# Attention and two MLPs in one kernel: q's two score parts made in place and carried by transfers, v's load later, a third column buffer

## The chip, the cores and the metric

The kernel runs on one core of a Trainium2 chip. The metric is the device time of one execution in microseconds; where several were taken, their median. A core has TensorE (PE, with its weight loads PEld), VectorE (DVE), ScalarE (ACT), GpSimd (POOL) and SyncE (SP), which here only issues transfers (DMAs). Each engine works through its own row of instructions in order; semaphores make one wait for another.

## The reference: what is computed

Rotary attention over 4 x 8 heads, 576 positions, 64 numbers a head, and two MLPs over the 2304 rows that it gives:

```python
q_rot, k_rot = (rotate(q), rotate(k))
scores = scale * np.matmul(q_rot, k_rot.transpose(0, 1, 3, 2))      # scale = 1/8
attn = np.exp(scores - np.max(scores, axis=-1, keepdims=True))
attn = attn / (np.sum(attn, axis=-1, keepdims=True) + 1e-09)
x = np.matmul(attn, v)                              # -> 2304 x 512
...
h = x @ w_in
g = np.where(h >= 1, h, np.where(h <= -1, 0.0, (h + 1) ** 2 / 4))
x = g @ w_out                                       # 512 -> 2048 -> 512
...
g = s * np.maximum(x @ w_in2, 0.0) ** 2 + b
out = g @ w_out2
```

## The kernel before

**Pairs and units.** Two heads share the 128 partitions, 64 each, so the 32 heads make 16 pairs. A pair is worked through in 9 units (`UNITS`). A unit makes scores of 128 rows by 576 columns on TensorE (`qk`, L352) in one of two score buffers (`ps_s`, `sc`), VectorE takes the row maximum (L354, `nm`), ScalarE the exponential (L359, `p`), which frees the score buffer. Two units later TensorE transposes `p` (L374), and later multiplies it with v (`av`).

**Two parts.** The scores are made with 32-bit numbers cut in two: a high part that TensorE takes as it is, and the rest. For q, both parts of a head stand above each other in one tile `qs` of 128 partitions: high part of head 0 in the lower half, its rest in the upper half, and for head 1 the other way round. Beside it stands k: `kh` holds k's high part twice, `kz` its rest.

**q before the change** (`rope_pair`, `lay_q`): the load `qin` brings q and its swapped halves side by side (`t[:, 0]`, `t[:, 1]`). GpSimd multiplies both by the table of cosines and sines (L96, in four pieces), VectorE adds them (L293). Then for each head, on its 64 partitions, ScalarE writes the scaled high part straight into `qs` (L306), and VectorE the rest into the other half of `qs` (L307): two instructions on each engine for a pair. There are two `qs` tiles, used in turn, so these writes wait until the scores two pairs earlier have been made.

**k** already goes the way that q takes after the change: parts are made in place in `kin` (L318 on ScalarE, L96 on GpSimd), and six transfers of 64 partitions on SP carry them to `kh` and `kz` (L323, L324).

**What sets the order.** Four buffers (`QB`) hold `qin` and `kin`; the one of a pair is loaded again for the pair two later. The code names in which unit a step is asked for (`do_load`): q of the next pair in unit 0, k in unit 2, v in unit 3, the loads of q and k for the pair after it in units 4 and 6. The framework's scheduler then sorts each engine's row by a time line of its own, so a step can stand far from there. All transfers are issued by SP, in one row: one that has to wait holds all behind it.

**Beside the pairs.** From about the fourth pair on, ScalarE, VectorE and GpSimd convert the weights of the first MLP from raw 64-bit form (`wraw`, L144, L133 to L138), and from the sixth pair on chunks of that MLP run beside the pairs (`beside`, L180): their columns come through the buffers `xs` (`split_x`), of which there are two. After the last pair the MLP stages fill the rest of the span.

Of the kernel before, what the change touches and what calls it, by code (L numbers as in the profile page):

```python
# [8 lines left out]
F32 = mybir.dt.float32  # L9
F32R = mybir.dt.float32r  # L10
# [3 lines left out]
AF = mybir.ActivationFunctionType  # L14
ALU = mybir.AluOpType
# [8 lines left out]
P = 128  # L24
# [37 lines left out]
N1 = 288  # L62
# [4 lines left out]
def kernel(ctx, tc, qq, kk, vv, tab, ww1, ww2, s, b, out):  # L67
    nc = tc.nc
# [31 lines left out]
    def split(dst_hi, dst_lo, src, hi_eng, lo_eng):  # L100
        if hi_eng is nc.scalar:
            made.append(nc.scalar.copy(dst_hi, src).ins)
        else:
            hi_eng.tensor_copy(dst_hi, src)
        tt = pool_tt if lo_eng is nc.gpsimd else nc.vector.tensor_tensor
        tt(out=dst_lo, in0=src, in1=dst_hi, op=ALU.subtract)  # L106
# [7 lines left out]
    class Slice:  # L114
# [6 lines left out]
        def convert(self, raw, pools, hi, lo):  # L121
            if not wide:
                split(hi, lo, raw, nc.scalar, nc.gpsimd)
                return


            top = raw.bitcast(F32).rearrange("p (n t) -> p n t", t=2)[:, :, 1]
            low = raw.bitcast(U16).rearrange("p (n t) -> p n t", t=4)[:, :, 1]
            pool = pools[self.f * 2 + self.made & 1 if len(pools) > 1 else 0]
            a = pool.tile([P, HW], F32, tag="wa", name="wa", bufs=WB)  # L130
            m = pool.tile([P, HW], F32, tag="wm", name="wm", bufs=WB)
            au, mu = a.bitcast(U32), m.bitcast(U32)
            nc.scalar.activation(a, top, AF.Copy, scale=2.0 ** -112)  # L133
            nc.vector.tensor_scalar(out=mu, in0=au, scalar1=3, scalar2=None, op0=ALU.logical_shift_left)
            nc.vector.scalar_tensor_tensor(out=mu, in0=au, scalar=0x80000000, in1=mu, op0=ALU.bitwise_and, op1=ALU.bitwise_or)
            nc.vector.tensor_scalar(out=au, in0=mu, scalar1=0xFF800000, scalar2=None, op0=ALU.bitwise_and)
            nc.vector.scalar_tensor_tensor(out=a, in0=low, scalar=2.0 ** -36, in1=a, op0=ALU.mult, op1=ALU.mult)
            nc.scalar.copy(hi, m)  # L138
            pool_tt(out=m, in0=m, in1=hi, op=ALU.subtract)
            pool_tt(out=lo, in0=m, in1=a, op=ALU.add)  # L140
# [95 lines left out]
    m2 = p1.enter_context(tc.tile_pool(name="m2", bufs=2, reuse_waits="tile"))  # L236
# [20 lines left out]
    def load_qk(i, nm, pieces=WHOLE):  # L257
        bb, hp = divmod(i, NP)
        t = att2.tile([P, 2, S], F32, tag="qkin", name=f"{nm}in", bufs=QB)
        for c in pieces:  # L260
            nc.sync.dma_start(out=t[:, :, c], in_=(qq if nm == "q" else kk)[bb, hp, :, :, c])
        qk_in[nm, i] = t

    def load_v(i):
        bb, hp = divmod(i, NP)
        t = att2.tile([P, 5, 2, D], F32, tag="vin", name="vin", bufs=VB)
        for out, src in ((t[:, :, 1], vv[bb, hp, :, :, 1]), (t[:D, :4, 0], vv[bb, hp, D:, :4, 0]), (t[D:, :4, 0], vv[bb, hp, :D, 1:, 0]), (t[D:, 4, 0], vv[bb, hp, :D, 0, 0])):
            nc.sync.dma_start(out=out, in_=src)
        v_in[i] = t
# [7 lines left out]
    QW = S + 2 * D  # L277
# [7 lines left out]
    def rope_pair(i, nm, mul, add, lo_eng, pieces=WHOLE):  # L285

        t = qk_in.pop((nm, i))
        tt = {nc.gpsimd: pool_tt, nc.vector: nc.vector.tensor_tensor}
        last = None
        for c in pieces:  # L290
            tt[mul](out=t[:, :, c], in0=t[:, :, c], in1=tab_sb[:, :, c], op=ALU.mult)
            r = t[:, 1, c]
            tt[add](out=r, in0=t[:, 0, c], in1=r, op=ALU.add)  # L293
            last = (lay_q if nm == "q" else lay_k)(i, t, c, lo_eng)
        return last

    SELF = [slice(0, D), slice(D, P)]

    def lay_q(i, t, c, lo_eng, heads=range(2)):

        st = stacks["q", i] = qs_t[i % 2]
        r = t[:, 1, c]
        for j in heads:
            own, other = SELF[j], SELF[1 - j]
            at = slice(j * QW + c.start, j * QW + c.stop)
            h = nc.scalar.activation(st[own, at], r[own], AF.Copy, scale=0.125)  # L306
            m = nc.vector.scalar_tensor_tensor(out=st[other, at], in0=r[own], scalar=0.125, in1=st[own, at], op0=ALU.mult, op1=ALU.subtract)  # L307
        return h.ins, m.ins
# [144 lines left out]
    def load_parts(x, n0, n):  # L453

        for t in range(2):
            nc.sync.dma_start(out=x[t].bitcast(F32), in_=parts_at(t, n0, n))
        return x

    def split_x(c, again):
        xh = m1.tile([P, KD, N1], F32R, tag="xh", name="xh")  # L460
        xl = m1.tile([P, KD, N1], F32R, tag="xl", name="xl")
        if again:
            return load_parts((xh, xl), c * N1, N1)
        for k in range(KD):
            xs = m2.tile([P, N1], F32, tag="xs", name="xs", bufs=2)
            nc.sync.dma_start(out=xs, in_=xd[k, :, c * N1:(c + 1) * N1])
            split(xh[:, k, :], xl[:, k, :], xs, nc.scalar, nc.gpsimd)
        return xh, xl

    kept, begun = set(), set()  # L470

    def beside(work):
        x = split_x(work[0][0], work[0][0] in kept)
        for _ in range(LEAD):
            yield 1.0
        for n, (c, gi) in enumerate(work):
# [12 lines left out]
            if n + 1 < len(work) and work[n + 1][0] != c:  # L489
                x = split_x(work[n + 1][0], work[n + 1][0] in kept)  # L490
# [27 lines left out]
    def turned_by(t, c):  # L518
        nc.vector.tensor_tensor(out=t[:, :, c], in0=t[:, :, c], in1=tab_sb[:, :, c], op=ALU.mult)
        nc.vector.tensor_tensor(out=t[:, 1, c], in0=t[:, 0, c], in1=t[:, 1, c], op=ALU.add)  # L520
# [5 lines left out]
    lay_k(0, tk, HALVES[1], [nc.gpsimd, nc.gpsimd], [0])  # L526
    turned_by(tq, QP[0])
    hi, rest = lay_q(0, tq, QP[0], None, [0])
    with tc.issue_after(hi):
        first = lay_k(0, tk, HALVES[1], [nc.gpsimd, nc.gpsimd], [1])  # L530
    hi, rest = lay_q(0, tq, QP[0], None, [1])
    with tc.issue_after(first):
        load_qk(1, "k")
# [37 lines left out]
    def do_load(n):  # L571
        if n < 2:
            with tc.issue_after(maxs[0] if n else rest):
                turned_by(tq, QP[n + 1])
                lay_q(0, tq, QP[n + 1], None)
        if n < len(units):
            i, k = units[n]
            if i + 1 < NPAIR:
                if k == (i == 0):
                    with ExitStack() if i else tc.issue_after(maxs[1]):  # L580
                        rope_pair(i + 1, "q", nc.gpsimd if i else nc.vector, nc.vector, None)
                elif k == 2:
                    with ExitStack() if i else tc.issue_after(exps[2]):
                        rope_pair(i + 1, "k", nc.gpsimd, nc.gpsimd, [nc.gpsimd, nc.vector])
                elif k == 3:
                    load_v(i + 1)
                elif k in (4, 6) and i + 2 < NPAIR:
                    load_qk(i + 2, "q" if k == 4 else "k")

        if n in range(33, 51, 2) or n in range(70, 110, 4):  # L590
            with tc.issue_after(exps[n - 14]):
                convert()

        if n in PARK_AT and parking:
            with tc.issue_after(exps[n - 4]):
                parking.pop(0).park(wst, scratch)()
# [31 lines left out]
    def do_fill(n):  # L628
        if n < 48:
            return  # L630
        with tc.issue_after(exps[min(n, len(units)) - 4]):
            run_fill(0.62 if n < 76 else 0.92)

    acts = {"q": do_qk, "l": do_load, "t": do_t, "a": do_av, "f": do_fill}
    for n in range(len(units) + LA):
        with ExitStack() as st:
# [377 lines left out]
    def cut(n0, n1, n):  # L1014

        k = -(-(n1 - n0) // n)
        at = [n0 + (n1 - n0) // 16 * i // k * 16 for i in range(k + 1)]
        return [(a, b - a) for a, b in zip(at, at[1:])]
# [5 lines left out]
    a, b, c, d = cut(last, NT, N2A), cut(0, last, N2), cut(last, NT, N2), cut(0, NT, N2)  # L1024
# [153 lines left out]
```

## Time and profile before

| | |
|---|---|
| three runs | 1129.34, 1130.87, 1133.84 us; median 1130.87 |
| the profiled execution | 1128.27 us; its span 1126.5 us |
| PE busy | 1077.9 us (96%) |
| PEld busy | 986.6 us (88%) |
| DVE busy | 780.8 us (69%) |
| ACT busy | 631.7 us (56%) |
| POOL busy | 429.5 us (38%) |
| DMA queue of SP | 48.9% of 16 engines' span |

The span runs from the first to the last instruction of the profiled execution; the execution's own time has 1.8 us more around it. Busy shares are means over stages that have different limits, and a matmul's end is modelled, so a busy TensorE is not one at its peak. The pairs fill about the first 440 us.

### The profile page before, as it was taken

Reading aid. Unit: us, or ns where it says so; the run is one execution under the profiler, and the core shown is the slowest. Engines: PE = TensorE matmul, PEld = TensorE weight load, DVE = VectorE, ACT = ScalarE, POOL = GpSimd, SP = SyncE. Lnnn points to the kernel's source line nnn. Section 1 sums busy time; section 2 is a strip of 40 time slices with the busy share of each in tenths; the row PEclk is TensorE's granted clock in tenths of the full one; section 3 lists DMA queues with packets and bytes.
Section 4 is the critical chain, followed back from the end, with each engine's and each line's share of the span. In section 5 each row is a group of like instructions: output and inputs, shape, how many; then the busy total and the mean of one; then the engine's idle time right before and its main releaser. Section 6 shows DMA issues by size and latency. Waiting matters only on the chain.

```text
span 1126.5 us, 20041 instructions
## 1 busy us (share of the span) xinstructions
PE 1077.9 (96%) x7296; PEld 986.6 (88%) x7296; DVE 780.8 (69%) x1449; ACT 631.7 (56%) x1430; POOL 429.5 (38%) x564
## 2 busy tenths in 40 slices
PE   3999998989999999999999999999999999999998
PEld 3666677878988989999999999999999999999997
DVE  6888987775676663365656667766877678767754
ACT  4777776775766765554545545465444448334421
POOL 7969886885453241252544444310211120000000
PEclk9999998999999999999999999999999999999999
DMA  7565855665667552745466673322232754221220
GB/s 228 164 180 165 243 158 182 213 170 177 186 193 216 174 182 76 262 130 187 141 221 222 193 234 113 118 77 88 80 126 90 274 182 126 82 70 54 81 62 35
DMA packets 109762, 173.24 MB, mean 154 GB/s; under 512 B 29408, under 2 KB 80608, under 8 KB 109664
## 3 DMA queue, kind: packets, MB, share of 16 engines
q1 hardware_dynamic: 109664, 171.97, 48.9%
q8 instruction: 57, 0.93, 0.3%
q14 instruction: 41, 0.34, 0.1%
HBM read 110.10 MB, written 48.56 MB: 141 GB/s over the span
## 4 chain that ended last, share of the span: by engine, by line
PE 77%; DVE 5%; DMA 5%; POOL 4%; ACT 3%; issue 2%; SPq 1%; POOLq 0%; ACTq 0%
PE hps L180 15%; PE sum L914 13%; PE yps L830 6%; PE yps L828 6%; PE yps L829 6%; PE sc L352 5%; PE h L180 4%; PE yps L764 4%; PE yps L766 4%; PE yps L765 4%; PE y L180 4%; PE av L400 3%; PE tp L374 3%; POOL kin L96 2%; DMA kin<-in_k 1%
## 5 line engine op out<-in xcount | busy, mean ns | idle before, releaser
L180 PE MATMUL hps<-xh,w 128*128 128x288 f32 (+4 forms) x640 | 163.3, 324 | 0.0
L354 DVE TENSOR_REDUCE nm<-sc 128x1 f32<-128x576 f32 x144 | 107.9, 752 | 43.2 <-PE sc L352 42.5
L352 PE MATMUL sc<-kh,qs 128*128 128x288 f32 x336 | 104.7, 333 | 28.5 <-ACT p L359 16.6
L359 ACT ACTIVATE p<-sc,nm 128x576 f32<-128x576 f32 x144 | 106.8, 744 | 33.5 <-DVE nm L354 32.6
L830 PE MATMUL yps<-gh,w 128*128 128x480 f32 (+1 forms) x320 | 118.5, 370 | 0.0
L828 PE MATMUL yps<-gh,w 128*128 128x480 f32 (+1 forms) x320 | 118.4, 370 | 0.0
L829 PE MATMUL yps<-gl,w 128*128 128x480 f32 (+1 forms) x320 | 118.4, 370 | 0.0
L922 ACT ACTIVATE four<-four,b_sb,s_sb 128x480 f32<-128x480 f32 x64 | 47.4, 782 | 126.3 <-DVE four L921 126.3
L96 POOL TENSOR_TENSOR wm<-wm,w 128x256 f32<-128x256 f32 x80 | 71.3, 912 | 120.1 <-ACT w L138 74.2
L180 PEld LDWEIGHTS hps<-xh,w 128*128 128x128 f32 x640 | 113.3, 188 | 1.0
L352 PEld LDWEIGHTS sc<-kh,qs 128*128 128x128 f32 x336 | 65.2, 197 | 47.9 <-ACT p L359 24.5
L180 PE MATMUL hps<-xl,w 128*128 128x288 f32 (+4 forms) x320 | 103.6, 324 | 0.0
L352 PE MATMUL sc<-kz,qs 128*128 128x288 f32 x336 | 95.9, 305 | 0.0
L374 PE MATMUL tp<-ident,p 128*128 128x128 f32 x576 | 89.4, 280 | 5.4 <-ACT p L359 3.3
L764 PE MATMUL yps<-gh,w 128*128 128x288 f32 (+3 forms) x288 | 93.2, 324 | 1.1 <-ACT ys L502 0.5
L766 PE MATMUL yps<-gh,w 128*128 128x288 f32 (+3 forms) x288 | 92.8, 322 | 0.0
L765 PE MATMUL yps<-gl,w 128*128 128x288 f32 (+3 forms) x288 | 92.8, 322 | 0.0
L96 POOL TENSOR_TENSOR wm<-wm,raw 128x256 f32<-128x256 f32 x16 | 12.8, 818 | 175.6 <-ACT raw L138 175.6
L374 PEld LDWEIGHTS tp<-ident,p 128*128 128x128 f32 x576 | 72.1, 144 | 8.5 <-ACT p L359 3.7
L180 PE MATMUL y<-gh,w 128*128 128x288 f32 x320 | 74.4, 304 | 3.5 <-ACT pt L377 1.7
L180 PE MATMUL h<-xh,w 128*128 128x288 f32 x320 | 74.0, 308 | 3.3 <-DVE gl L106 2.6
L400 PE MATMUL av<-pt,vin 128*64 128x256 f32 (+1 forms) x512 | 75.1, 417 | 0.2
(154 smaller groups left out, 2886.5 us busy)
## 6 DMA issues: line engine op xcount, KB each, us to landing
wraw<-in_ww SPq DMA_DIRECT2D x56, 512.0 KB, 4.1
w<-parkd SPq DMA_DIRECT2D x24, 512.0 KB, 6.3
kin<-in_k SPq DMA_DIRECT2D x15, 576.0 KB, 5.2
qin<-in_q SPq DMA_DIRECT2D x15, 576.0 KB, 4.1
kh<-kin SPq DMA_DIRECT2D x60, 144.0 KB, 2.7
parkd<-wraw SPq DMA_DIRECT2D x16, 512.0 KB, 2.9
xs<-y1d SPq DMA_DIRECT2D x32, 240.0 KB, 2.7
xd<-u SPq DMA_DIRECT2D x16, 288.0 KB, 2.6
```

The lines of the kernel that those rows point to most:

```text
L180: m = nc.tensor.matmul(out_ps, l, r, start=(i == 0), stop=(i == n - 1))
L352: nc.tensor.matmul(sc[:, half, o:o + n], l, r[:, k0:k0 + n], start=m == 0, stop=m == len(todo) - 1)
L354: maxs[i * 9 + k] = nc.vector.tensor_reduce(out=nm, in_=sc[:, :, :288], axis=AX.XY, op=ALU.max, negate=True).ins
L374: m = nc.tensor.transpose(v[:, c, :], p[:, c * P:(c + 1) * P], ident)
L400: nc.tensor.matmul(ps[j * D:(j + 1) * D, :n], v[:, kt, j, :], pt[g][:, kt, j, :], start=kt == 0, stop=False)
L764: nc.tensor.matmul(acc, wh, gh, start=f == 0, stop=False)
L765: nc.tensor.matmul(acc, wh, gl, start=False, stop=False)
L766: nc.tensor.matmul(acc, wl, gh, start=False, stop=last)
L828: nc.tensor.matmul(acc, wh, gh, start=f == 0, stop=False)
L829: nc.tensor.matmul(acc, wh, gl, start=False, stop=False)
L830: nc.tensor.matmul(acc, wl, gh, start=False, stop=last)
L914: nc.tensor.matmul(acc, l, r, start=j == 0, stop=j == len(t) - 1)
```

## The change

From the third pair on (`i > 1`), q's two parts are made in place in its load buffer: one ScalarE copy of 128 partitions into `t[:, 0]` (L305 after the change), one VectorE instruction of 128 partitions for the rest into `t[:, 1]` (L306), and four transfers of 64 partitions on SP to the four quarters of `qs` (L310). The load of v for the next pair is asked for in unit 7 instead of 3, and `xs` has three buffers instead of two. Line numbers behind the inserted lines grow by 9.

```diff
         st = stacks["q", i] = qs_t[i % 2]
         r = t[:, 1, c]
+        if i > 1:
+            hi, lo = t[:, 0, c].bitcast(F32R), r.bitcast(F32R)
+            nc.scalar.activation(hi, r, AF.Copy, scale=0.125)
+            nc.vector.scalar_tensor_tensor(out=lo, in0=r, scalar=0.125, in1=t[:, 0, c], op0=ALU.mult, op1=ALU.subtract)
+            for j in heads:
+                at = slice(j * QW + c.start, j * QW + c.stop)
+                for part in range(2):
+                    m = nc.sync.dma_start(out=st[SELF[j ^ part], at].bitcast(F32), in_=t[SELF[j], part, c])
+            return m.ins
         for j in heads:
...
-            xs = m2.tile([P, N1], F32, tag="xs", name="xs", bufs=2)
+            xs = m2.tile([P, N1], F32, tag="xs", name="xs", bufs=3)
...
-                elif k == 3:
+                elif k == 7:
                     load_v(i + 1)
```

The scheduler sorts the rows anew. This is VectorE's row before, in the second half of the sixth pair (pair 5) up to the first unit of the next; each `L354` is one unit's row maximum. The second `L307` of this turn stands three rows behind the last one shown:

```order
L381 COPY pt<-tp 128x4x128
L293 TENSOR_TENSOR qin<-qin 128x576
L436 TENSOR_TENSOR u<-av,r 128x256
L354 TENSOR_REDUCE nm<-sc 128x1 x2
L381 COPY pt<-tp 128x4x128
L415 RECIPROCAL sume<-sume 128x5
L354 TENSOR_REDUCE nm<-sc 128x1
L392 COPY ptr<-tr 128x384
L354 TENSOR_REDUCE nm<-sc 128x1
L307 SCALAR_TENSOR_TENSOR qs_108<-qin,qs_108 64x576
L354 TENSOR_REDUCE nm<-sc 128x1
```

And the same stretch of the row with the change, where `L363` is the row maximum and `L306` the new subtraction:

```order
L363 TENSOR_REDUCE nm<-sc 128x1
L445 TENSOR_TENSOR u<-av,r 128x256
L363 TENSOR_REDUCE nm<-sc 128x1
L390 COPY pt<-tp 128x4x128
L293 TENSOR_TENSOR qin<-qin 128x576
L424 RECIPROCAL sume<-sume 128x5
L363 TENSOR_REDUCE nm<-sc 128x1
L401 COPY ptr<-tr 128x384
L306 SCALAR_TENSOR_TENSOR qin<-qin 128x576
L363 TENSOR_REDUCE nm<-sc 128x1 x2
```

The add (L293) has moved two row maxima back. The rest of q (L307 before, twice at the turn of the pair) is one instruction now, one row maximum behind the add. Over pairs 2 to 12 the add moves by 0, 1 or 2 row maxima, one on average; the subtraction stands in the same unit as the add or one later.

This is SP's row before at the turn from the third pair to the fourth, where k of pair 4 is carried to its tiles (`kz_109`, `kh`) and q and k of pair 6 are loaded:

```order
L442 DMA xd<-u 128x576
L324 DMA kz_109<-kin 64x576
L466 DMA xs<-xd 128x288
L323 DMA kh<-kin 64x576 x4
L324 DMA kz_109<-kin 64x576
L261 DMA qin<-in_q 128x1152
L261 DMA kin<-in_k 128x1152
L144 DMA wraw<-in_ww 128x512
L268 DMA vin<-in_v 128x5x64
```

And the same turn with the change, where `L310` carries q's parts and `L332` and `L333` are k's:

```order
L451 DMA xd<-u 128x576
L268 DMA vin<-in_v 64x64
L310 DMA qs_107<-qin 64x576 x2
L333 DMA kz_109<-kin 64x576
L310 DMA qs_107<-qin 64x576 x2
L332 DMA kh<-kin 64x576 x4
L333 DMA kz_109<-kin 64x576
L144 DMA wraw<-in_ww 128x512
L261 DMA qin<-in_q 128x1152
L475 DMA xs<-xd 128x288
L261 DMA kin<-in_k 128x1152
L268 DMA vin<-in_v 128x5x64
```

Four transfers have come in ahead of the load of q, and the load of raw weights (`wraw`), which stood behind both loads, stands ahead of q's here. v's loads stand where they stood, behind `kin` and around `xd`. At the later turns `wraw` stands ahead of q's parts, ahead of k's parts or between the two loads in at least three more places.

## Rows read from the trace of the kernel before

**Rows 1.** Stages: length; PE, PEld, DVE, ACT, POOL busy (instructions); clock; DMA share; GB/s.
```profile
56.00:140.00 84.00, 77.03 (x564) 55.18 (x563) 73.06 (x122) 61.50 (x143) 66.89 (x90) 1.00 0.68 194
140.00:293.00 153.00, 138.06 (x1017) 119.88 (x1016) 117.17 (x204) 104.48 (x254) 108.05 (x142) 0.96 0.61 181
293.00:440.00 147.00, 145.07 (x1136) 129.75 (x1135) 95.85 (x179) 98.64 (x244) 60.71 (x90) 1.00 0.56 171
440.00:1126.00 686.00, 681.61 (x4367) 653.97 (x4365) 454.71 (x883) 333.14 (x714) 146.43 (x176) 1.00 0.42 136
```

**Rows 2.** Chain that ended last, 56 to 293 us: shares by line.
```profile
by line: PE sc L352 9.2%; issue 8.5%; POOL kin L96 7.4%; DMA kin<-in_k 6.4%; PE h L180 5.3%; PE tp L374 4.9%; PE av L400 4.6%; DVE nm L354 4.5%; PE y L180 4.3%; DMA kz<-kin 3.5%; ACT p L359 3.4%; DVE qs L307 3.0%; POOL qin L96 2.9%; DMA qin
```

**Rows 3.** Groups, 40 to 440 us: count | busy, mean ns | idle before.
```profile
L307 DVE SCALAR_TENSOR_TENSOR qs<-qin,qs 64x576 fp32r<-64x576 f32 x26 | 24.7, 951 | 1.9 <-ACT qs L306 1.1
...
L293 DVE TENSOR_TENSOR qin<-qin 128x576 f32<-128x576 f32 x12 | 13.9, 1160 | 10.1 <-POOL qin L96 10.1
...
L306 ACT ACTIVATE qs<-qin 64x576 fp32r<-64x576 f32 x26 | 17.8, 684 | 2.1 <-PE sc L352 1.5
...
L318 ACT CAST kin<-kin 128x576 fp32r<-128x576 f32 x13 | 8.7, 671 | 3.8 <-POOL kin L96 3.6
```

**Rows 4.** Tile qs alone, 56 to 293 us: PE, PEld, DVE, ACT, POOL busy.
```profile
56.00:293.00 237.00, 71.49 (x378) 54.11 (x378) 17.97 (x19) 12.29 (x18) 0.00 (x0) 0.97 0.63 186
```

**Rows 5.** Tile qs, whole span, L307: shortest/median/longest ns, then first and last start.
```profile
L307 DVE SCALAR_TENSOR_TENSOR qs<-qin,qs x36: 286/754/2304, 11.2 to 380.8; 64x576 fp32r<-64x576 f32 x30, 64x128 fp32r<-64x128 f32 x2, 64x160 fp32r<-64x160 f32 x2, 64x288 fp32r<-64x288 f32 x2
```

**Rows 6.** Waits of the engines, 56 to 293 us: total us, times, longest.
```profile
POOL qin L96 <- DMA qin<-in_q: 17.5, 7, 7.3
...
DVE qin L293 <- POOL qin L96: 6.9, 5, 3.1
```

**Rows 7.** Chain that ended last, 114 to 132 us: start us, us, what.
```profile
116.27 3.25 DMA kz<-kin
...
119.60 4.84 DMA kin<-in_k
...
125.07 0.81 POOL qin L96
...
125.91 1.27 DVE qin L293
...
127.51 0.68 DVE nm L354
```

**Rows 8.** Row maxima (L354) alone, 56 to 140 us: length, DVE busy (instructions).
```profile
56.00:140.00 84.00, 27.06 (x37) 1.00 0.68 194
```

**Rows 9.** SP's row in time, turn of a pair: start us, us, transfers issued.
```profile
113.76 2.41 SPq L323 DMA_DIRECT2D kh<-kin  x4
```

**Rows 10.** DMA issues, whole span: count, KB each, median us to landing.
```profile
qin<-in_q SPq DMA_DIRECT2D x15, 576.0 KB, 4.1
kh<-kin SPq DMA_DIRECT2D x60, 144.0 KB, 2.7
...
xd<-u SPq DMA_DIRECT2D x16, 288.0 KB, 2.6
```

**Rows 11.** SP's waits, 56 to 293 us: total us, times, longest.
```profile
SPq L144 <- DVE wa L137: 40.5, 11, 8.6
SPq L466 <- POOL xl L96: 16.5, 7, 7.8
SPq L268 <- PE rm L428: 15.7, 4, 7.3
```

**Rows 12.** Stretches around the clock's falls, columns as in rows 1.
```profile
180.00:186.00 6.00, 4.00 (x32) 3.76 (x30) 4.15 (x7) 3.65 (x8) 4.82 (x9) 1.00 0.44 126
186.00:198.00 12.00, 10.79 (x62) 8.96 (x63) 9.20 (x18) 8.86 (x22) 5.65 (x8) 0.72 0.45 116
246.00:252.00 6.00, 4.93 (x24) 4.68 (x25) 5.31 (x10) 5.98 (x16) 4.99 (x7) 0.72 0.43 106
276.00:282.00 6.00, 6.00 (x38) 5.98 (x37) 3.33 (x8) 3.88 (x11) 3.23 (x6) 0.73 0.43 163
```

## Prediction

> **What bounds the kernel now.** I read the busy time of every engine by stage first, because the share over the whole span mixes stages with different limits. From 440 us on, TensorE is busy for 681.61 of 686 us, and from 293 to 440 us for 145.07 of 147 [rows 1]. There the matmuls of the two multilayer stages cover everything else, and nothing that VectorE, ScalarE or a queue saves can shorten the run. Of the sixteen pairs, the reader should therefore look at those that run between 56 and 293 us. In 56 to 140 VectorE is busy for 73.06 of 84 us (87%), TensorE for 77.03; in 140 to 293 VectorE has 117.17 of 153 us and TensorE 138.06, so TensorE lacks 7 and 15 us. (The first 56 us belong mostly to the start and to pairs 0 and 1, which the change leaves alone.)
>
> Next I read the chain of work that ended last, for 56 to 293 us [rows 2]. It changes hands all the time: scores on TensorE, POOL's rotation of k, the load of k, VectorE's row maxima, ScalarE's exponentials. No engine owns the stage. What owns it is a loop: a score tile must be reduced by VectorE and exponentiated by ScalarE before one of only two score buffers is free, and VectorE and ScalarE work strictly in their written order, so anything put between two units delays the loop. VectorE's q parts (L307) are 3.0% of that chain: 7.1 of 237 us.
>
> **The change, part by part.**
>
> *Two parts in place.* For pairs 2 to 15 (14 pairs), two ScalarE copies and two VectorE subtractions over 64 partitions become one of each over 128. Of L307, 26 lie in 40 to 440 us, at a mean of 0.951 us; ScalarE's L306 takes 0.684, and the nearest 128-partition copy (L318, k's) takes 0.671 [rows 3]. So twice as many partitions cost the same time, and I price the new instructions like the old: VectorE is relieved of 14 x 0.951 = 13.3 us, ScalarE of 28 x 0.684 - 14 x 0.671 = 9.8. From 56 to 293 us these instructions hold VectorE for 17.97 and ScalarE for 12.29 us [rows 4]; half goes, 9.0 and 6.1. How much lies on the path? VectorE has 7.1 of 17.97 us on the chain, so halving gives **3.6 us**; bounds are 0 (all in slack) and 9.0. ScalarE's L306 is below the part of the chain's list that can be read; I take **1.0 us**, between 0 and 40% of 6.1, or 2.4. What is saved after 293 us I count at nothing: TensorE covers it.
>
> On VectorE and GpSimd together: most L307 take 0.75 us, but the longest 2.304 [rows 5], and L293, which adds q's halves, takes 1.160 on average [rows 3], both in stretches where GpSimd runs. The Trainium skill (SBUF — State Buffer, Who interferes with whom) says that a VectorE instruction with two SBUF inputs and a GpSimd instruction that reads SBUF exclude each other for their whole length. The trace's spread agrees with that. By that rule each instruction removed also gives GpSimd up to 0.75 us, 10.5 us in all; GpSimd's two rotation lines have 7.4% and 2.9% of the chain, so a tenth of it, 1 us, would come on top. I leave it out, since the mean of 0.951 already carries the collisions as VectorE sees them.
>
> *The place in the rows.* The order of VectorE shows the add (L293), which needs GpSimd's product, about one unit later than before (two at the place shown), and the subtraction one reduce behind it, not at the turn of the pair. The add now waits 6.9 us for GpSimd and GpSimd 17.5 us for the load of q [rows 6]. The chain around 120 us shows that wait passing on: a transfer of kz, the load of k, GpSimd's q, the add, and only then the next row maximum [rows 7]. A unit in 56 to 140 us is 84 / 37 = 2.3 us [rows 8]; against it q's load comes later, because the four new transfers stand ahead of it on SP. Four like them, kh's, take 2.41 us to issue [rows 9]. At two units' shift the wait goes, at one it stays about even, so I take **2 of the 6.9 us** as won; bounds are 6.9 won and the loss of rival C. In exchange ScalarE's copy now waits for the add directly, and VectorE's subtraction for that copy; between add and subtraction stands one reduce, which covers the 0.67 us of the copy. Where it doesn't, 0.67 us a pair is lost.
>
> *Four transfers.* They move 576 KB a pair. A kh transfer of that form lands 2.7 us after its issue [rows 10]. That is hidden: SP writes q's tiles when the scores two pairs earlier are done with them, and they are read a whole pair (nine units, some 20 us) later. Without that cover each pair would start about 2.7 us late, 14 times.
>
> *v later.* v's first issue waits up to 7.3 us on SP for the last readers of its buffer [rows 11]. But the order shows v at the same place of SP's row as before, behind kin and ahead of xd, which waits for the same group's end anyway. I count 0; bounds are 0 and, if xs behind it matters, a gain of 1.
>
> *Third column buffer.* SP waits 16.5 us in 7 waits for GpSimd to free an xs tile [rows 11], with kz, kh and the loads queued behind. They have a pair's slack except the load of q, so I take **0.5 us** of gain; bounds are 0 and 2.
>
> **Sum.** 3.6 + 1.0 + 2.0 + 0.5 = 7.1 us off the profiled execution, 1128.27 -> 1121.2. That execution is 2.6 us under the median of the three runs, 1130.87, so the forecast is 1130.87 - 7.1 = 1123.8, **1124 us** (0.6% faster). A difference of about 0.5%, 5.7 us, is what a measurement of this kernel can tell from none.
>
> **Rivals.**
>
> *B, relieved but covered (about 1128.5).* The chain goes through every engine in this stage [rows 2]. A neighbour that is nearly as late takes over: TensorE is already busy for 215 of 237 us [rows 1]. If half of the first two terms and none of the others arrive, the gain is 2.3 us. For it speaks that no engine has over 3% of the chain in these lines; against it, VectorE's 87%.
>
> *C, the load of q comes too late (slower, about 1139).* The order of SP shows a load of raw weights (wraw) ahead of q's load, where it stood behind k's. This load waits for VectorE's conversion: 40.5 us in 11 waits, 3.7 each, up to 8.6 [rows 11]. Then q is late by 3.7 + 2.4 = 6.1 us, less one unit of 2.3 makes 3.8, and VectorE waits that long at the add with every later row maximum behind it, ScalarE at its copy with the exponentials behind it. I see the wraw at such a place (ahead of q's parts, k's parts or q's load) in about four pairs: 4 x 3.8 = 15 us against the gain of 7.1, so 1130.87 + 8 = 1139. It decides from (7.1 + 5.7) / 4 = 3.2 us a pair on. Against it: where these waits are long, it is because VectorE is late itself, and it is relieved now; and of the waits so far only 6.9 us reached VectorE.
>
> On the four transfers, kh's of 144 KB over 64 partitions lands in 2.7 us and xd's of 288 KB over 128 in 2.6 [rows 10], so a half costs as much as a whole. The Trainium skill (the same page, "Can I just issue two DMAs to hit both halves?") says that two such halves serialize. By that rule the four would cost as much as 1152 KB ahead of q's load: q's 576 KB lands in 4.1 us [rows 10], 1.4 more than 144 KB, so 0.47 for each 144 KB and 3.7 us for the four, not the 2.4 of SP's issue. C would cost 1.3 us a pair more, 5 in all.
>
> *D, the clock holds as well (about 1117).* The granted clock falls from 2.4 to 1.2 GHz three times in this stage, the longest time right after six microseconds in which TensorE was busy for 4.00. The three stretches of 12, 6 and 6 us with a mean of 0.72, 0.72 and 0.73 lose at most 3.4 + 1.7 + 1.6 = 6.7 us [rows 12]. If the shorter waits keep them away, A's gain doubles: 1130.87 - 13.8 = 1117. New idle stretches could as well bring another one, 1.7 to 3.4 us each; so I count none in the sum.
>
> **Chances and range.** A (forecast, 1119 to 1128) 0.42, B 0.33, C 0.13, D 0.12. Faster by over 0.5%: D and four fifths of A, 0.46. Within 0.5%: B and the rest of A, 0.41. Slower: C, 0.13. The range from 1115 to 1136 holds A, B, nearly all of D and the milder half of C. A alone would be 1119 to 1128.
>
> **What would show it.** Right: in 56 to 293 us L307 is gone, one L306 of about 0.75 to 0.95 us a pair stands in its place, VectorE's busy time there falls by about 9 us and ScalarE's by 6, the add's wait for GpSimd is under 6.9 us, no score matmul waits for a q transfer, and the second layer stages start about 7 us sooner with the rest unchanged. Wrong: VectorE idles longer at the add or at the subtraction, GpSimd waits more than 17.5 us for q's load, SP's wraw waits stand ahead of q's load (rival C), or VectorE's and ScalarE's time falls as said and TensorE's idle time doesn't (rival B).

## The result, and the profile after

The changed kernel takes 1145.12 us (median of 4 runs, 1142.84 to 1146.74) against 1130.11 us for the kernel before, run beside it (4 runs, 1126.44 to 1133.84). The ratio is 1.0142 with a 95% interval of 1.0120 to 1.0163: it is slower, by about 15 us, where I had forecast 6 to 7 us faster, and it lies outside the range of 1115 to 1136 us that I had given. The profiled execution took 1146.74 us, its span 1144.7.

Where in the span the time went shows in the row of the row maxima, which mark the units: count, shortest, median and longest in ns, then the start of the first and of the last. This is the kernel before:

```profile
L354 DVE TENSOR_REDUCE nm<-sc x144: 719/757/759, 14.4 to 432.1; 128x1 f32<-128x576 f32 x144
```

And the changed kernel:

```profile
L363 DVE TENSOR_REDUCE nm<-sc x144: 711/757/760, 14.4 to 448.7; 128x1 f32<-128x576 f32 x144
```

The last unit starts 16.6 us later, so the pairs hold nearly all of the 18.5 us that lie between the two profiled executions. The stages of the changed kernel, with the columns of rows 1:

```profile
56.00:140.00 84.00, 75.57 (x535) 53.45 (x535) 68.39 (x116) 58.27 (x139) 67.17 (x91) 0.98 0.78 220
140.00:293.00 153.00, 133.75 (x963) 116.58 (x960) 106.23 (x185) 94.91 (x234) 107.67 (x140) 0.93 0.64 186
293.00:440.00 147.00, 140.95 (x1092) 124.20 (x1090) 88.91 (x168) 92.76 (x231) 63.03 (x89) 1.00 0.66 198
440.00:1126.00 686.00, 683.77 (x4413) 655.71 (x4412) 456.71 (x893) 340.59 (x737) 146.94 (x178) 1.00 0.41 135
```

VectorE and ScalarE are less busy than in [rows 1], as forecast, but TensorE is too: it did fewer instructions in the same stretches. Up to 440 us GpSimd alone is a little fuller (by 2.3 us from 293 us on); TensorE, VectorE and ScalarE wait longer. The groups that answer to [rows 3], 40 to 440 us:

```profile
L306 DVE SCALAR_TENSOR_TENSOR qin<-qin 128x576 fp32r<-128x576 f32 x13 | 14.8, 1141 | 1.8 <-ACT qin L305 1.8
L293 DVE TENSOR_TENSOR qin<-qin 128x576 f32<-128x576 f32 x12 | 13.4, 1115 | 14.5 <-POOL qin L96 14.5
...
L327 ACT CAST kin<-kin 128x576 fp32r<-128x576 f32 x13 | 8.7, 672 | 10.6 <-POOL kin L96 10.0 <-DMA qs<-qin 0.5
L305 ACT ACTIVATE qin<-qin 128x576 fp32r<-128x576 f32 x12 | 8.2, 685 | 16.3 <-DVE qin L293 16.3
```

ScalarE's two halves of 17.8 us became one copy of 8.2, as priced. VectorE's 24.7 us became 14.8. The new figure is behind the last bar: ScalarE stood idle for 16.3 us right ahead of its copy, waiting for VectorE's add, and VectorE stood idle for 14.5 us ahead of the add, waiting for GpSimd (10.1 before). Ahead of k's copy ScalarE waited 10.0 us, 3.6 before. The engines' waits from 56 to 293 us, to be laid beside [rows 6]:

```profile
POOL qin L96 <- issue: 18.8, 3, 10.5
...
ACT qin L305 <- DVE qin L293: 12.1, 7, 2.6
...
DVE qin L293 <- POOL qin L96: 8.5, 6, 2.7
...
POOL qin L96 <- DMA qin<-in_q: 6.9, 2, 4.9
...
POOL qin L96 <- DMA xs<-xd: 5.0, 1, 5.0
...
POOL qin L96 <- DMA wraw<-in_ww: 4.8, 2, 3.9
```

Part of GpSimd's wait ahead of q's products is now put down to other releasers, but the load stands behind it: in pairs 5 to 15 GpSimd's first product starts 3.9 to 7.4 us after the load was issued and at most 0.25 us after it landed. Taken together, whatever releaser is named, these waits come to 35.5 us (18.8 + 6.9 + 5.0 + 4.8), twice the 17.5 us of before, so this sign of being wrong came true. SP's row at the turn to the sixth pair shows why the load is late (start us, us, what it issued):

```profile
115.16 1.15 SPq L310 DMA_DIRECT2D qs<-qin  x2
116.40 0.55 SPq L333 DMA_DIRECT2D kz<-kin  x1
117.05 1.18 SPq L310 DMA_DIRECT2D qs<-qin  x2
119.51 0.33 SPq L144 DMA_DIRECT2D wraw<-in_ww  x1
119.90 2.43 SPq L332 DMA_DIRECT2D kh<-kin  x4
...
123.65 0.82 SPq L261 DMA_DIRECT2D qin<-in_q  x1
```

The pair's first row maximum starts at 120.6 us, q's load 3.1 us behind it. For the eleven adds of pairs 5 to 15 I took the start of the load less that of the nearest pair's first row maximum: the mean is -0.2 us before and +2.3 us with the change. What the lateness does to the rows shows at 340 to 354 us (start us, us, instruction; in brackets the idle time ahead of it and its releaser):

```profile
341.50 0.75 DVE L363 TENSOR_REDUCE nm<-sc 128x1 f32<-128x576 f32 x1
...
343.29 3.07 POOL L96 TENSOR_TENSOR qin<-qin,tab_sb 128x288 f32<-128x288 f32 x4 [4.39 <-DMA qin<-in_q]
...
346.38 0.76 DVE L293 TENSOR_TENSOR qin<-qin 128x576 f32<-128x576 f32 x1 [4.14 <-POOL qin L96]
347.06 0.42 DVE L134 TENSOR_SCALAR wm<-wa 128x512 uint32<-128x512 uint32 x1
347.18 0.68 ACT L305 ACTIVATE qin<-qin 128x576 fp32r<-128x576 f32 x1 [2.81 <-DVE qin L293]
...
348.96 1.36 DVE L306 SCALAR_TENSOR_TENSOR qin<-qin 128x576 fp32r<-128x576 f32 x1
...
352.39 0.74 DVE L363 TENSOR_REDUCE nm<-sc 128x1 f32<-128x576 f32 x1
```

The load lands late, GpSimd's four products follow, VectorE's add has stood at the head of its row for 4.14 us, ScalarE's copy for 2.81 us, and the next row maximum comes 10.9 us after the last one, where a unit takes 3.0 us on average ((448.7 - 14.4) / 143).

The granted clock followed. Its mean over 56 to 293 us is 0.95, 0.97 before [rows 4]. A mean of 0.95 is a tenth of 237 us at 1.2 GHz, or up to 11.9 us of TensorE's time; 0.97 is 7.1. So up to some 5 us of the loss go with the clock. I take its fall for a consequence of the waits; no run separates the two.

### The profile page after: what moved, and what is told of

Its sections match the earlier page's. It is cut to its first block, busy times and chain, and to the rows that moved or that the text cites. A ratio compares the mean times of both kernels' runs of the same rounds, so it can differ in the third digit from the quotient of the medians.

```text
span 1144.7 us, 20117 instructions
## 1 busy us (share of the span) xinstructions
PE 1084.7 (95%) x7296; PEld 990.2 (86%) x7296; DVE 768.2 (67%) x1435; ACT 622.3 (54%) x1416; POOL 431.6 (38%) x564
## 4 chain that ended last, share of the span: by engine, by line
PE 75%; DMA 7%; DVE 6%; POOL 5%; ACT 3%; issue 2%; SPq 2%; POOLq 0%; DVEq 0%; ACTq 0%
PE hps L180 15%; PE sum L923 13%; PE yps L838 6%; PE yps L839 6%; PE yps L837 5%; PE sc L361 4%; PE yps L773 4%; PE y L180 4%; PE yps L775 4%; PE yps L774 4%; PE av L409 4%; PE h L180 3%; POOL kin L96 3%; PE tp L383 3%; DMA kin<-in_k 2%
## 5 line engine op out<-in xcount | busy, mean ns | idle before, releaser
L363 DVE TENSOR_REDUCE nm<-sc 128x1 f32<-128x576 f32 x144 | 108.0, 752 | 53.0 <-PE sc L361 52.5
```

## The experiments

Each line of "measured" gives the median, its runs' range, and the ratio to the kernel before, run beside it (medians of before in the four sets of runs: 1128.75, 1128.92, 1128.97 and 1128.72 us). The square brackets hold the ratio's 95% interval.

**Which part of the change costs.** Two kernels: only q's new way (column buffers and v as before), and only the other two edits.

```diff
 q_alone, against the changed kernel (v_xs_alone: the other way, against the kernel before)
-            xs = m2.tile([P, N1], F32, tag="xs", name="xs", bufs=3)
+            xs = m2.tile([P, N1], F32, tag="xs", name="xs", bufs=2)
...
-                elif k == 7:
+                elif k == 3:
                     load_v(i + 1)
```

> q's new way alone, v in unit 3 and two column buffers as before. Theory 1 (the four transfers make the load of q late, and the add, ScalarE's copy and the subtraction wait in a row behind it) and theory 2 (the copy and the subtraction stand too close behind the add, whatever the load does): 1141 to 1149 us, as the whole change (1145), with the load of q issued some 2 us after the turn of a pair and ScalarE waiting over 10 us for the add. Theory 3 (v's and xs's edits, or the new order as such, cost the time): 1127 to 1134.

> The two small edits alone, q made as before. Theories 1 and 2: 1127 to 1134 us, as before. Theory 3: 1139 to 1146.

Measured: q_alone 1141.87 us (1140.54 to 1143.03), ratio 1.0123 [1.0095, 1.0151]. v_xs_alone 1125.84 us (1124.12 to 1130.10), ratio 0.9981 [0.9966, 0.9996]. The loss is q's new way; the other two edits win about 2 us together, with a granted clock that was also higher (a mean of 0.996 over their runs, 0.993 over those of the kernel before beside them).

**The transfers, away and added.** The changed kernel without its four transfers, and the kernel before with four transfers of the same size a pair from `qs` to spare DRAM.

```diff
 no_transfers, against the changed kernel
-                    m = nc.sync.dma_start(out=st[SELF[j ^ part], at].bitcast(F32), in_=t[SELF[j], part, c])
-            return m.ins
+            return
 more_transfers, against the kernel before, behind the loop over heads
+        if i > 1:
...
+                    nc.sync.dma_start(out=spare[j, part], in_=st[SELF[j ^ part], at].bitcast(F32))
```

> The whole change without its four transfers: q's parts are made in place, but pairs 2 to 15 make their scores from the q of pairs 0 and 1, so the output is not the reference's. Theory 1: 1118 to 1130 us, the load of q no later than before. Theory 2: 1138 to 1148, with ScalarE still waiting over 10 us for the add.

> The kernel before with four more transfers of 144 KB a pair, out of q's score tiles into a spare place in memory; no engine's work changes, and q's load buffer is not held by them. Theory 1, if issuing and moving them is enough: 1138 to 1150 us, q's load 2 us later against the turn. Theory 1, if it takes the buffer that they hold: 1129 to 1135. Theory 2: 1128 to 1133, no change.

Measured: no_transfers 1134.92 us (1132.83 to 1138.73), ratio 1.0072 [1.0042, 1.0102]; ScalarE's copy still waits 13.6 us in 7 waits for the add (56 to 440 us). more_transfers 1134.40 us (1133.63 to 1138.50), ratio 1.0065 [1.0043, 1.0088]; q's load came 2.6 us behind the turn. By these ratios the transfers cost 7 to 8 us in either kernel (0.70% of it taken away from 1.42%, 0.65% added), and without them the changed kernel, with less work on two engines, is still slower than the kernel before. Neither cause alone was enough, and neither kernel came out where theory 1 had it if issuing and moving them is enough. The first figure is the weaker one: in no_transfers the scheduler also drew q's steps forward, so that the add of pair 15 stands in the eleventh pair and not in the thirteenth, and SP's loads of q and k wait for the subtraction instead (13.9 us in 4 waits, 56 to 440 us).

**Bytes or SP's row.** more_transfers again, with 4 columns a transfer instead of 576.

```diff
-nc.sync.dma_start(out=spare[j, part], in_=st[SELF[j ^ part], at].bitcast(F32))
+nc.sync.dma_start(out=spare[j, part, :, :4], in_=st[SELF[j ^ part], at][:, :4].bitcast(F32))
```

> The kernel before with the same four extra transfers a pair as in more_transfers, at the same place of SP's row, but of 4 columns each instead of 576: SP issues them and waits as there, and they carry next to nothing. If it is the issue and the waits in SP's row that make q's load late: 1133 to 1137 us, like more_transfers. If it is the 576 KB that they move: 1127 to 1131 us, like the kernel before.

Measured: 1136.62 us (1134.68 to 1137.53), ratio 1.0065 [1.0039, 1.0091], the same as with 144 KB each. Its issues of this kind (count, KB, median us to landing), and its wait for q's load from 56 to 440 us, with that of the kernel before:

```profile
spare<-qs SPq DMA_DIRECT2D x56, 1.0 KB, 2.2
```

```profile
POOL qin L97 <- DMA qin<-in_q: 33.2, 9, 9.0
```

```profile
POOL qin L96 <- DMA qin<-in_q: 20.3, 9, 7.3
```

The load is 2.7 us behind the turn here too, with a hundredth of the bytes. So it isn't the bytes: four more issues, and their waits for the parts that they carry, stand ahead of q's load in SP's row. How much of the cost is these and how much the rows that the scheduler sorted anew around them isn't separated; in more_transfers and more_tiny alike the add stands one to three row maxima later than in the kernel before, in nine of eleven pairs.

**The place of copy and subtraction.** The changed kernel with both ordered behind the turn at which q's parts stood before; the same without the transfers; and the same with the transfers issued by GpSimd.

```diff
 turn_parts, against the changed kernel
+            with tc.issue_after(exps[9 * (i - 2) + 7]):
                 nc.scalar.activation(hi, r, AF.Copy, scale=0.125)
                 nc.vector.scalar_tensor_tensor(out=lo, in0=r, scalar=0.125, in1=t[:, 0, c], op0=ALU.mult, op1=ALU.subtract)
 turn_no_transfers: this, and no four transfers
 turn_pool: this, and
-                    m = nc.sync.dma_start(out=st[SELF[j ^ part], at].bitcast(F32), in_=t[SELF[j], part, c])
+                    m = nc.gpsimd.dma_start(out=st[SELF[j ^ part], at].bitcast(F32), in_=t[SELF[j], part, c])
```

> The changed kernel, with the copy and the subtraction ordered behind the turn of the pair, where q's parts stood before, so that four to six units lie between the add and them; the four transfers stay. Theory 2 (the add, the copy and the subtraction, set close behind one another, stop both engines' rows; price about 6 us): 1132 to 1140 us, and the copy's wait for the add falls from 16 us to under 4. Theory 1 alone (only the transfers' delay of q's load counts, the place costs nothing): 1142 to 1148 us.

> As turn_parts, and without the four transfers, so that q's parts never reach the score tiles from the third pair on (output not the reference's); the halved work of VectorE and ScalarE stays. If the transfers and the close chain are all that the change costs, what is left is the gain that I had forecast for the halved work: 1120 to 1128 us. If a third cost is in it (the subtraction over 128 partitions colliding with GpSimd, say): 1131 us or more.

> As turn_parts, but GpSimd issues the four transfers in its own row, so that SP's row holds nothing new ahead of the loads; the bytes are the same. If SP's row is how the transfers cost time: 1122 to 1131 us. If the bytes cost it: as turn_parts. If GpSimd, which then waits in its row for the subtraction, falls behind with the rotations of k and q: over 1138 us, with the wait of its q products growing.

Measured: turn_parts 1136.32 us (1135.10 to 1139.79), ratio 1.0072 [1.0047, 1.0097]; turn_no_transfers 1133.21 us (1130.19 to 1135.87), ratio 1.0040 [1.0024, 1.0057]; turn_pool 1163.43 us (1162.80 to 1164.65), ratio 1.0303 [1.0273, 1.0332]. Moving the two instructions away wins about 8 us (0.70%), as theory 2 said, and ScalarE's wait for the add is gone. (The turn in question is the second one behind the add, some 12 to 15 units on; the four to six units in the expectation count only to the first.) But turn_no_transfers, which has neither cause, falls short of its forecast by 5 us or more. Its add waits 16.1 us for GpSimd where the kernel before has 10.1 (56 to 440 us). My reading is that the work that VectorE no longer does stood between the turn and the add, and VectorE now only comes to the add sooner. turn_pool came out as its third case had it, so it says nothing on SP's row. Its transfers take GpSimd's row, and GpSimd waits there for ScalarE's copy too (groups, 40 to 440 us):

```profile
L311 POOL DMA_DIRECT2D qs<-qin x56 | 29.6, 532 | 11.8 <-ACT qin L306 6.5 <-ACT ys L512 3.0 <-DVE qin L307 2.2
```

**The add alone, later.** This gave a fourth theory: load, products and add form a chain that starts at the turn, and VectorE's row stops at whichever place the add has been given ahead of that chain's end. The parts made from it are carried to the score tiles only at the end of the following pair. So I ordered the add behind a later row maximum, for pairs 5 to 15, in four kernels: the sixth row maximum of the pair that runs (unit 5 in the code) in late_tnt (from turn_no_transfers), late_turn (from turn_parts) and late_vx (from v_xs_alone), the eighth in late_after (from the changed kernel). The edit of late_after (for the sixth, 5 stands in place of 7):

```diff
-            tt[add](out=r, in0=t[:, 0, c], in1=r, op=ALU.add)
+            with tc.issue_after(maxs[9 * (i - 3) + 7]) if nm == "q" and i > 4 else ExitStack():
+                tt[add](out=r, in0=t[:, 0, c], in1=r, op=ALU.add)
```

> As turn_no_transfers (output not the reference's), with the add of q's halves ordered behind the sixth row maximum of its pair instead of the third to fifth, for pairs 5 to 15. Theory 4: the time that VectorE saves between the turn and the add is given back at the add, which stands ahead of GpSimd's product, and load, rotation and add are a chain from the turn of the pair on; then a later add brings the saving out: 1122 to 1129 us, and the add's wait falls from 16 us to under 6. If the wait at the add only goes elsewhere (another engine's chain is as late): 1131 to 1135 us.

> As turn_parts (copy and subtraction at the turn, with the four transfers), with the add ordered behind the sixth row maximum as in late_tnt. Theory 4: the transfers' later load of q reaches VectorE only through the add's wait (16.7 us in turn_parts), so most of that goes and the time falls from 1136 to 1126 to 1132 us. If the load's delay takes effect in another way (GpSimd's row, k's rotation behind q's, the clock): 1134 to 1138 us.

> As v_xs_alone (q as before, v later, third column buffer), with the add ordered behind the sixth row maximum as in late_tnt. Theory 4: the add's wait of 9.3 us falls to under 4 us and some of it is won: 1120 to 1125 us. If this wait costs nothing on its own: 1124 to 1128 us.

> The changed kernel, with the add ordered behind the eighth row maximum of its pair for pairs 5 to 15; copy and subtraction then stand one to two units behind it, at the turn. If the close chain behind a late GpSimd is what the changed kernel pays beside the transfers, moving the add alone mends it: 1130 to 1138 us, with the copy's wait for the add under 5 us. If the copy must stand further from the add (as in turn_parts): 1141 to 1147 us.

Measured: late_tnt 1126.89 us (1124.26 to 1131.47), ratio 0.9985 [0.9968, 1.0002]; late_turn 1133.61 us (1132.07 to 1138.70), 1.0051 [1.0035, 1.0068]; late_vx 1125.56 us (1123.30 to 1128.62), 0.9975 [0.9955, 0.9995]; late_after 1124.90 us (1123.17 to 1128.66), 0.9960 [0.9946, 0.9974]. With the add alone ordered later, the changed kernel goes from 1.42% slower to 0.40% faster than the kernel before, with all four transfers in it. I had allowed 1130 to 1138 us for it. late_turn lies between its two ranges, and so settles neither. The groups of late_after, 40 to 440 us, and its row maxima:

```profile
L294 DVE TENSOR_TENSOR qin<-qin 128x576 f32<-128x576 f32 x12 | 12.9, 1077 | 0.0
L307 DVE SCALAR_TENSOR_TENSOR qin<-qin 128x576 fp32r<-128x576 f32 x13 | 12.7, 975 | 0.8 <-ACT qin L306 0.8
...
L306 ACT ACTIVATE qin<-qin 128x576 fp32r<-128x576 f32 x12 | 8.3, 688 | 1.7 <-DVE qin L294 1.5
```

```profile
L364 DVE TENSOR_REDUCE nm<-sc x144: 714/757/760, 14.6 to 429.0; 128x1 f32<-128x576 f32 x144
```

The add's wait went from 14.5 us to nothing and the copy's from 16.3 to 1.5, and the last unit starts 19.7 us sooner. Yet q's load is as late as before, 2.9 us behind the turn: the lateness is still there, and neither VectorE's add nor ScalarE's copy of q stands against it any more. ScalarE's copy of k waits 14.3 us for GpSimd (10.0 us in the changed kernel, 3.6 before), but in late_vx, where q's load is on time, it waits 15.9, so that wait is not the load's alone. late_vx wins nothing measurable over v_xs_alone, where the wait was smaller (9.3 us).

**What is left for the change itself.** late7_vx has q the old way and the add at the place of late_after; late7_turn is late_turn with the add there. The edit is the one above.

> As v_xs_alone (q's parts written by halves, as before), with the add behind the eighth row maximum, the same place as in late_after. If late_after owes its time to the halved work of VectorE and ScalarE, this is slower than it by 2 us or more: 1127 to 1130 us. If it owes it to the add's place alone: 1123 to 1126 us, level with it.

> As late_turn, with the add behind the eighth row maximum instead of the sixth. In late_turn the load of q was still 4 us behind the turn, and the add met GpSimd's product without slack in four of eleven pairs. If that is what is left of the cost: 1123 to 1128 us. If the transfers cost time by themselves where copy and subtraction stand at the turn: 1132 to 1135 us, as late_turn.

Measured: late7_vx 1122.93 us (1120.90 to 1124.61), ratio 0.9953 [0.9936, 0.9970]; late7_turn 1131.16 us (1128.79 to 1135.05), 1.0024 [1.0007, 1.0041]. late7_vx, with the lowest median of all, doesn't have q's new way, and its interval overlaps that of late_after: with the add out of the way, halved work on two engines plus four transfers bring nothing that can be measured. It ran beside the kernel before and not beside the changed one; by the two ratios it is 1.9%, some 21 us, shorter than that.

late7_turn met neither forecast. In its profile the eleventh pair starts at 252.8 us, in late_after's at 252.9, so up to there the transfers cost it nothing; the twelfth starts at 285.2 against 283.7 and the thirteenth at 325.1 against 318.7. What lies between (start us, us, instruction):

```profile
291.42 0.42 SPq L261 DMA_DIRECT2D qin<-in_q  x1
292.01 0.33 SPq L261 DMA_DIRECT2D kin<-in_k  x1
292.39 0.49 SPq L166 DMA_DIRECT2D parkd<-wraw  x1
...
298.82 3.05 POOL L96 TENSOR_TENSOR qin<-qin,tab_sb 128x288 f32<-128x288 f32 x4 [6.97 <-DMA qin<-in_q]
...
306.48 0.67 ACT L329 CAST kin<-kin 128x576 fp32r<-128x576 f32 x1 [4.00 <-POOL kin L96]
```

q's load was issued at 291.4 us and took 7.2 us to land; in late_after it was issued at 288.3 and took 5.4. Behind it SP issued the load of k and a store of converted weights (`parkd`). GpSimd's products of q stood still until the load had landed, its work on k came behind them, and ScalarE waited 4.00 us at its copy of k with the next exponentials behind it. The stretches that follow, with the columns of rows 1:

```profile
306.00:312.00 6.00, 4.34 (x23) 3.38 (x22) 2.37 (x6) 4.01 (x11) 2.63 (x6) 0.87 0.71 223
312.00:318.00 6.00, 5.59 (x26) 4.86 (x25) 3.27 (x8) 4.34 (x11) 0.79 (x1) 0.57 0.25 65
```

TensorE was busy for 4.34 of six microseconds, and the granted clock fell to a mean of 0.57; in late_after it was 1.00 in both stretches. By these means the clock alone lost up to 3.4 us. In this one execution that place holds most of the difference; whether it does in all the runs of this kernel wasn't tried.

## Why the prediction was wrong

**Two parts in place.** The relief was there: ScalarE's part as priced (17.8 to 8.2 us), VectorE's mis-sized. I priced the subtraction over 128 partitions like one over 64, 0.951 us; it took 1.141 on average, so 26 x 0.951 became 13 x 1.141 and 9.9 us were saved from 40 to 440 us, not 12.4. The 3.6 and 1.0 us of it that I put on the path did not arrive. turn_no_transfers suggests where they went: VectorE came to the add earlier and waited there. That is rival B's mechanism, with GpSimd's q as the neighbour that takes over.

**The place in the rows: the step that failed.** I wrote that "ScalarE's copy now waits for the add directly" and priced behind it only VectorE's wait for the copy, 0.67 us a pair, which did stay small (1.8 us in all). ScalarE's own wait for the add I left without a price, although I had named it and had named in rival C the exponentials behind it. It was 12.1 us from 56 to 293 us, and in late_after, where the add stands later and this wait is nearly gone, so is the loss. For the add itself I took 2 of 6.9 us as won; its wait grew to 8.5 us. The add did stand about one unit later, and the load was later by 2.6 us, close to the 2.4 that I had worked out against a unit of 2.3. So "about even" was nearly right for VectorE, and the win beside it had nothing to rest on.

**Four transfers.** That the score tiles have a pair's slack was right: no score matmul waits for a transfer of q. But hidden they were not, since q's load stands behind them in SP's row: more_transfers and more_tiny price that at about 7 us in the kernel before. I had the delay, in the step above, and not its price. The sum by the Trainium skill (SBUF — State Buffer, "Can I just issue two DMAs to hit both halves?"), by which the bytes of the half-width transfers would add 5 us in all, is not borne out: the extra stores of more_tiny cost the same as those of more_transfers with a hundredth of the bytes. That was tried with stores to DRAM, not with the change's own transfers into `qs`.

**v later and the third column buffer.** 0.5 us forecast, about 2 measured (0.9981), of which the higher clock can be all.

**The rivals.** C had the right sign and the right start, a late load of q with VectorE and ScalarE standing in their rows behind it, and 1139 us against 1145. Its cause was only partly right. Raw weights stand shortly ahead of q's load at three turns (at 81.8, 119.5 and 176.9 us), and SP stood idle ahead of them for at most 1.3 us, not for 3.7; SP's wait for VectorE's conversion, 40.5 us in [rows 11], fell to 17.7. The four transfers stand ahead of the load in every pair. Its counterargument, that "only 6.9 us reached VectorE", missed that the change lets the same lateness reach ScalarE as well. D's reverse came true: the mean of the granted clock fell from 0.97 to 0.95.

**What is shown, and what is not.** Shown: where the add stands decides the whole loss, since moving it alone (with copy and subtraction behind it) gives back all of it; and q's new way is worth nothing measurable with the add there. Not separated: how much of late_after's gain is VectorE's and how much ScalarE's, since its copy moved along with the add. Open is also why late7_turn, with the add at the same place and the copy and the subtraction further behind, is 6 to 7 us slower than late_after. The repairs tried one at a time (turn_parts and no_transfers, 0.70% each) don't add up to turn_no_transfers (1.02%), which fits two ways of shortening the same wait better than two independent prices.

The granted clock of every run is on record too. An estimate of what it took at most is the span times what its mean lacks to 1: 11.7 us in the changed kernel (mean 0.990), 4.3 in late_after (0.996), 8.6 in the kernel before beside late_after (0.992). So some 7 of the 20 us between the changed kernel and late_after go with the clock, and the 0.40% by which late_after is ahead of the kernel before may be the clock alone. In no_transfers and late_turn, too, the clock takes 5 to 6 us more than in the kernel before, most of what each is slower. Whether the waits brought the clock down was not tried.

## What to carry to other kernels

When an edit delays a load, look for the first instruction in each in-order row that needs its product, and ask when that product is used at all: here an add whose result is carried on more than a pair later stood ahead of row maxima that everything waited for. A new dependence between two engines must be priced on both, as a wait of the engine that is handed the work too. And work saved just ahead of a wait may be no gain, as here; order the waiting instruction later first, and then see whether the saving is worth anything.

## What the runs showed of the hardware

The time of a transfer in the issuing row hardly depended on its size: two of more_tiny's 1 KB took SP 1.10 us at the turn to the sixth pair, two of more_transfers' 144 KB at the same place 1.10 too, two of the changed kernel's 144 KB 1.15 and 1.18. The small ones landed after 2.2 us, those of more_transfers after 2.7 (medians), and they cost the kernel the same. Issued from GpSimd, such a transfer took 0.53 us of its row.

The same subtraction, 128 x 576 on VectorE, took 0.71 to 1.38 us in the changed kernel, and its mean went with its place: 1.141 us close behind the add, where GpSimd works on k, 0.975 in late_after, 0.847 in turn_parts (11.0 us for 13). What decides is GpSimd's instruction of the moment. In the changed kernel the two shortest (0.71 and 0.74 us) started as one of k's had at most 0.05 us left to run, the five longest (1.30 to 1.38) as one of k's had 0.68 to 0.76 us left. It goes both ways: GpSimd's next instruction on k, begun beside the subtraction, took 1.30 to 1.42 us for twelve of the thirteen subtractions, where the shorter half of k's products took 0.78 to 0.81. So beside its work on k the subtraction held GpSimd for about 0.5 us a pair (an estimate from these times). The lines of [rows 5] had the same spread, and I should have taken the upper part of it for an instruction that was being moved next to GpSimd's work.
